# First block of a mixture layer with whole float32 products in place of split halves, on one Trainium2 core

## The chip, the cores and the metric

The kernel runs on one core of a Trainium2 chip. The metric is the device time of one execution in microseconds. Three runs of the kernel before gave 1545.82, 1546.03 and 1547.47 us, so its median is 1546.03 us.

## What is computed

Everything is float32. Attention comes first: keys and values are averaged over groups of 8 positions, so each of the 8 x 8 heads (576 queries, 64 wide) sees 72 keys. Its output is x, 4608 tokens by 512. Two feed-forward layers follow; the second takes the output of the first:

```python
h = np.maximum(np.maximum(x @ w1, x @ w2), x @ w3)   # 512 -> 768, three experts
y = h @ w_out                                        # 768 -> 512
h = np.maximum(y @ w_in, 0.0)                        # 512 -> 2048
return h * h @ w_out2                                # 2048 -> 512
```

The weights come from the host as 64-bit floats, read as pairs of 32-bit words.

## The kernel before, in words

**Split products.** A float32 operand is kept as two halves of the type float32r: hi is the operand rounded by a ScalarE (ACT) copy, lo the difference between the operand and hi. A product is then three float32r matmuls that add up in one PSUM bank, hi x hi, hi x lo and lo x hi (`PARTS`). The function `split` (L124, through `split_to`, L120) does it with one ACT copy (L121) and one subtraction (L122), on VectorE (DVE) or, where it is told so, on GpSimd (POOL).

**Weights of the first layer.** There are 24 weight tiles of 128 x 512: 18 for the three experts (`w1_t[f, e]`, 6 values of f, 3 experts) and 6 for the second product (`wo1_t[kk]`). The function `weights` (L161) makes each: `load_raw` (L128) loads 512 KB of 64-bit floats through SyncE's DMA queue into one of four buffers that turn in a ring (`place`, L113), `convert` (L136) makes float32 of it in a tile of three (tag "row") by two ACT operations (L148, L149) and two DVE operations (L150, L153), and `split` makes the halves, the subtraction on POOL. The raw buffers are shared with loads of keys (`load_k`) and values (`load_v`).

**The first layer by blocks.** The tokens go in 12 blocks of 384. `moe1(j)` (L453) makes one block in 22 steps: 18 steps (f, e) of 4 x 3 matmuls of 384 columns each (L465), with a running maximum over the experts (L471 on ACT, L473 on DVE) and a split of h after the third (L475); then 4 steps of 6 x 3 matmuls (L484), whose result goes out to DRAM (L490, L491). Three PSUM banks (`mm_ps`) serve these steps. The input of a block is four tiles x[kk], kk = 0 to 3, one for each pair of heads.

**Attention by pieces.** `attend` (L307) makes x for one pair and one run of tokens: load, `prepare` (q split, L330, on POOL for the first two blocks), `softmax` (L332: scores L344, maximum L346, exponentials L349, reciprocal L354, and a scaling on POOL, L355), `transpose` (L362: L370, and the halves of the transposed tile, L372 and L373), `values` (L375: L385 for the first batch, L395 to L399 for the others, ending with the split of x, L389 or L400).

**Order.** Each piece of work has a due time in steps in the list `todo`; `run` (L494) emits it in that order. A scheduler with a model of the chip then orders each engine's own instructions, so an engine takes them in an order fixed beforehand and waits at the head of its queue. Attention of block j is due before `moe1(j)` and beside `moe1(j-1)`. Weight loads of the first layer are due from step -12 on, 0.9 of a step apart:

```python
todo.append((0.9 * (NE * f + e) - 12, functools.partial(load_w1, f, e)))
todo.append((0.9 * (NE * KF1 + kk) - 12, functools.partial(load_wo1, kk)))
```

**The second layer.** Its weights are prepared during blocks 2 to 10 and stored in DRAM. From about 785 us on, the second layer runs alone (L600, L645).

Of the kernel before, what the change touches and what calls it, by code (L numbers as in the profile page):

```python
# [14 lines left out]
AF = mybir.ActivationFunctionType  # L15
ALU = mybir.AluOpType
# [4 lines left out]
P = 128  # L21
# [6 lines left out]
KD = DM // P  # L28
FF1 = 768
KF1 = FF1 // P  # L30
FF2 = 2048
KF2 = FF2 // P
NE = 3
# [7 lines left out]
PARTS = ((0, 0), (0, 1), (1, 0))  # L41
# [3 lines left out]
STEPS = NE * KF1 + KD  # L45
# [20 lines left out]
NATURAL = 1  # L66

LIGHT = 2

# [8 lines left out]
def as_f32(ap):  # L80
    return ap.bitcast(F32)
# [3 lines left out]
def attention_moe_kernel(ctx: ExitStack, tc: tile.TileContext, q, k, v, vn, w1, w2, w3, wo1, wi2, wo2, out):  # L85
    nc = tc.nc
# [11 lines left out]
    for sign, base in ((1, POOL * MID), (-1, POOL - 1 - POOL * MID)):  # L98
        nc.gpsimd.affine_select(
            out=sums, in_=sums, compare_op=ALU.is_ge, fill=0.0, base=base,  # L100
# [12 lines left out]
    def place(kind):  # L113
        if shared[0]:
            turns["both"] += 1
            return f"raw{turns['both'] % 4}"
        turns[kind] += 1
        return f"raw{2 * kind + turns[kind] % 2}"

    def split_to(hi, lo, src, engine):  # L120
        nc.scalar.activation(hi, src, AF.Copy)  # L121
        engine.tensor_tensor(out=lo, in0=src, in1=as_f32(hi), op=ALU.subtract)  # L122

    def split(hl, src, engine=nc.vector):  # L124

        split_to(hl[:, 0], hl[:, 1], src, engine)

    def load_raw(raw_pool, src, after=None):  # L128

        raw = raw_pool.tile([P, 512, 2], I32, tag=place(0), name="wraw", bufs=1)  # L130
        if after is not None:
            nc.gpsimd.tensor_copy(as_f32(raw[:1, 0, :1]), after[:1, :1])
        nc.sync.dma_start(out=raw.rearrange("p a b -> p (a b)"), in_=src.bitcast(I32))
        return raw

    def convert(raw_pool, raw, after=None):  # L136

        low, high = raw[:, :, 0], raw[:, :, 1]
        a = raw_pool.tile([P, 512], I32, tag="row", name="wbits", bufs=3)
        if after is not None:
            nc.gpsimd.tensor_copy(as_f32(a[:1, :1]), after[:1, :1])
        nc.scalar.activation(as_f32(a), as_f32(high), AF.Abs, scale=REBIAS)  # L148
        nc.scalar.activation(low, low.bitcast(U32), AF.Copy, scale=LOW_SCALE, bias=LOW_BIAS)  # L149
        nc.vector.scalar_tensor_tensor(  # L150
            out=a, in0=a, scalar=3, in1=low, op0=ALU.logical_shift_left, op1=ALU.bitwise_or
        )
        nc.vector.scalar_tensor_tensor(  # L153
            out=a, in0=high, scalar=-0x80000000, in1=a, op0=ALU.bitwise_and, op1=ALU.bitwise_or
        )
        return as_f32(a)
# [2 lines left out]
        return raw.rearrange("p a b -> p (a b)").rearrange("p (c a) -> p c a", c=2).bitcast(F32R)  # L159

    def weights(pool, raw_pool, src, name, tag=None):  # L161
        w = pool.tile([P, 2, 512], F32R, name=name, tag=tag or name)
        split(w, convert(raw_pool, load_raw(raw_pool, src)), nc.gpsimd)
        return w


    s1 = ctx.enter_context(ExitStack())
# [89 lines left out]
    x_t = {}  # L257
# [10 lines left out]
    def score_tiles(n):  # L268
        m = P if n % P == 0 else n // 2
        return [(c, m) for c in range(0, n, m)]  # L270

    def attention(j):

        x_t[j] = [None] * NPAIR
        n_tiles = sum(NPAIR * len(score_tiles(n)) for _, _, n, _ in pieces(j))
        pace = (STEPS - 1) / n_tiles
        at = (j - 1) * STEPS + pace / 2 - (LAG_T + LAG_V + LEAD_X)
        for b, s0, n, t in pieces(j):
            if s0 == 0 and b < NATURAL:
                tiles = []  # L280
                when = at - pace / 2 + LAG_T + LAG_V if t else at + pace / 2
                todo.append((when - LEAD_LOAD, lambda b=b, tiles=tiles: tiles.extend(load_natural(b))))
                todo.append((when, lambda tiles=tiles: pool_v(tiles)))
            for p in range(NPAIR):
                load, prepare, softmax, transpose, values = attend(j, b, s0, n, p, t)
                todo.append((at - LEAD_LOAD, load))
                todo.append((at - LEAD_PREP, prepare))
                tiles = score_tiles(n)
                if j < LIGHT:
                    todo.append((at, functools.partial(softmax, tiles)))  # L290
                for c, m in tiles:
                    if j >= LIGHT:
                        todo.append((at, functools.partial(softmax, [(c, m)])))
                    todo.append((at + LAG_T, functools.partial(transpose, c, m)))
                    at += pace
                todo.append((at - pace + LAG_T + LAG_V, values))
# [10 lines left out]
    def attend(j, b, s0, n, p, t):  # L307

        kr, vr, qr, qs, pt, sms = [], [], [], [], [], {}
        first, light = s0 == 0, j < LIGHT  # L310

# [63 lines left out]
        def values():  # L375
            if t == 0:
                x_t[j][p] = x_p.tile([P, 2, T1], F32R, tag="x", name="x")
            x = x_t[j][p][:, :, t : t + n]
            hi, lo = pt[0][:, 0, :, :n], pt[0][:, 1, :, :n]
            if b < NATURAL:  # L380
                av = av_ps.tile([P, T1], F32, tag="av0", name="av0")[:, :n]
                for i, (h, z, rhs) in enumerate(
                    (h, z, rhs) for h in range(2) for z, rhs in ((h, hi), (h, lo), (3 + h, hi))
                ):
                    nc.tensor.matmul(  # L385
                        av, lhsT=vst[:, p, z : z + 2].rearrange("p a d -> p (a d)"), rhs=rhs[:, h],
                        start=(i == 0), stop=(i == 5),
                    )
                split(x, av)  # L389
                return  # L390
            xf = xf_p.tile([P, T1], F32, tag="xf", name="xf")[:, :n]
            for h in range(2):
                av = av_ps.tile([P, T1], F32, tag=f"av{h}", name=f"av{h}")[:, :n]
                lhsT = vst[:, p, 2 * h : 2 * h + 2].rearrange("p a d -> p (a d)")
                nc.tensor.matmul(av, lhsT=lhsT, rhs=hi[:, h], start=True, stop=False)  # L395
                nc.tensor.matmul(av, lhsT=lhsT, rhs=lo[:, h], start=False, stop=True)  # L396
                r, o = slice(h * D, (h + 1) * D), slice((1 - h) * D, (2 - h) * D)
                nc.scalar.activation(xf[r], av[o], AF.Copy)
                nc.vector.tensor_tensor(out=xf[r], in0=av[r], in1=xf[r], op=ALU.add)  # L399
            split(x, xf)  # L400
# [3 lines left out]
    w1_t, wo1_t = {}, {}  # L404
# [47 lines left out]

    def moe1(j):  # L453

        x = x_t.pop(j)
        hs = []
        for f in range(KF1):
            hm = t_p.tile([P, T1], F32, tag="hm", name="hm")
            h = h_p.tile([P, 2, T1], F32R, tag="h", name="h")
            for e in range(NE):  # L460
                ps = mm_ps.tile([P, T1], F32, tag="ps", name="ps")
                n = 0
                for kk in range(KD):
                    for a, c in PARTS:
                        nc.tensor.matmul(  # L465
                            ps, lhsT=w1_t[f, e][:, a, kk * P : (kk + 1) * P], rhs=x[kk][:, c],
                            start=(n == 0), stop=(n == 3 * KD - 1),
                        )
                        n += 1
                if e == 0:  # L470
                    nc.scalar.activation(hm, ps, AF.Copy)  # L471
                else:
                    nc.vector.tensor_tensor(out=hm, in0=ps, in1=hm, op=ALU.max)  # L473
                if e == NE - 1:
                    split(h, hm)  # L475
                yield
            hs.append(h)
            now[0] = hm
        for d in range(KD):
            ps = mm_ps.tile([P, T1], F32, tag="ps", name="ps")  # L480
            n = 0
            for kk in range(KF1):
                for a, c in PARTS:
                    nc.tensor.matmul(  # L484
                        ps, lhsT=wo1_t[kk][:, a, d * P : (d + 1) * P], rhs=hs[kk][:, c],
                        start=(n == 0), stop=(n == 3 * KF1 - 1),
                    )
                    n += 1
            ys = t_p.tile([P, T1], F32, tag="ys", name="ys")
            nc.scalar.activation(ys, ps, AF.Copy)  # L490
            nc.scalar.dma_start(out=y_dram[j][d], in_=ys)  # L491
            yield
# [6 lines left out]
    def add_moe1(j):  # L499
        steps = moe1(j)  # L500
        todo.extend((j * STEPS + i, functools.partial(next, steps, None)) for i in range(STEPS))

    todo = []
# [3 lines left out]
            todo.append((0.9 * (NE * f + e) - 12, functools.partial(load_w1, f, e)))  # L507
    for kk in range(KF1):
        todo.append((0.9 * (NE * KF1 + kk) - 12, functools.partial(load_wo1, kk)))
    for j in range(NB1 - 1):  # L510
        add_moe1(j)
        attention(j + 1)
# [216 lines left out]
```

## Time and profile before

| | |
|---|---|
| median of three runs | 1546.03 us |
| the profiled execution, its own time | 1546.39 us |
| its span, first to last instruction | 1544.7 us |
| PE (TensorE matmul) busy | 1509.4 us, 98% |
| DVE busy | 948.2 us, 61% |
| ACT busy | 623.5 us, 40% |
| POOL busy | 199.4 us, 13% |
| DMA | 200.87 MB, mean 130 GB/s |

PE is the matmuls and PEld the weight loads into the array, which run beside them. A matmul's busy time contains the tail in which its results drain, so matmuls that follow each other closely overlap in the table of means, and a rate is better read from start to start or from a long unbroken run. PEclk is the granted clock of TensorE as a share of 2.4 GHz; 0.50 is 1.2 GHz. SPq is SyncE's queue of DMA issues. An arrow in the idle column names what ended the idle time. A wait for several things is put down to the one that came last.

### The profile page before, as it was taken

Reading aid. Unit: us, or ns where it says so; the run is one execution under the profiler, and the core shown is the slowest. Engines: PE = TensorE matmul, PEld = TensorE weight load, DVE = VectorE, ACT = ScalarE, POOL = GpSimd, SP = SyncE. Lnnn points to the kernel's source line nnn. Section 1 sums busy time; section 2 is a strip of 40 time slices with the busy share of each in tenths; the row PEclk is TensorE's granted clock in tenths of the full one; section 3 lists DMA queues with packets and bytes.
Section 4 is the critical chain, followed back from the end, with each engine's and each line's share of the span. In section 5 each row is a group of like instructions: output and inputs, shape, how many; then the busy total and the mean of one; then the engine's idle time right before and its main releaser. Section 6 shows DMA issues by size and latency. Waiting matters only on the chain.

```text
span 1544.7 us, 25098 instructions
## 1 busy us (share of the span) xinstructions
PE 1509.4 (98%) x9290; PEld 1413.8 (92%) x9290; DVE 948.2 (61%) x1991; ACT 623.5 (40%) x1772; POOL 199.4 (13%) x303
## 2 busy tenths in 40 slices
PE   6899999999999999999999999999999999999998
PEld 4789999999999999999999898988989888999987
DVE  6895678776776767755427555455655546464544
ACT  7875566656666556654212212121212112121211
POOL 5541122222222121322000000000000000000000
PEclk7799999999999999999999999999999999999999
DMA  7552234434334332323475424333333433343331
GB/s 226 159 172 68 76 105 149 145 95 143 122 119 143 97 132 99 102 77 123 135 289 208 150 109 164 110 121 123 112 137 124 150 123 108 111 150 109 137 109 69
DMA packets 80858, 200.87 MB, mean 130 GB/s; under 512 B 9024, under 2 KB 32576, under 8 KB 80736
## 3 DMA queue, kind: packets, MB, share of 16 engines
q1 hardware_dynamic: 73824, 189.83, 36.1%
q10 hardware_dynamic: 6912, 9.44, 1.7%
q8 instruction: 74, 1.21, 0.3%
q14 instruction: 48, 0.39, 0.1%
HBM read 157.29 MB, written 41.94 MB: 129 GB/s over the span
## 4 chain that ended last, share of the span: by engine, by line
PE 85%; DVE 5%; DMA 5%; ACT 2%; issue 2%; SPq 0%; POOL 0%; DVEq 0%; ACTq 0%; POOLq 0%
PE ps L465 25%; PE acc L645 25%; PE ps L600 21%; PE ps L484 9%; PE sc L344 2%; DMA out_dram<-o 2%; PE tr L370 2%; DMA wraw<-in_w_dram 1%; PE av L396 1%; PE av L395 1%; DVE wbits L153 1%; DMA vr<-in_v_dram 1%; DMA wraw<-in_wo_dram 1%; DMA kq<-in_k_dram 1%; DVE wbits L150 0%
## 5 line engine op out<-in xcount | busy, mean ns | idle before, releaser
L465 PE MATMUL ps<-x,w 128*128 128x384 f32 x2592 | 507.6, 343 | 1.8 <-DVE x L122 1.0
L465 PEld LDWEIGHTS ps<-x,w 128*128 128x128 f32 x2592 | 451.1, 191 | 3.9 <-DVE x L122 2.0
L645 PE MATMUL acc<-wo2s,g 128*128 128x512 f32 x1728 | 412.5, 391 | 0.0
L600 PEld LDWEIGHTS ps<-y,wi2s 128*128 128x128 f32 x3024 | 370.4, 188 | 12.5 <-PE ps L600 3.4
L600 PE MATMUL ps<-y,wi2s 128*128 128x256 f32 x3024 | 376.8, 280 | 2.8 <-DVE s L629 2.2
L645 PEld LDWEIGHTS acc<-wo2s,g 128*128 128x128 f32 x1728 | 316.2, 188 | 62.6
L121 ACT ACTIVATE g<-c 128x512 fp32r<-128x512 f32 x144 | 90.8, 630 | 410.4 <-DVE c L611 403.6
L617 DVE TENSOR_TENSOR s<-ps,s 128x512 f32<-128x512 f32 x72 | 49.8, 692 | 262.2 <-PE ps L600 261.6
L484 PE MATMUL ps<-h,wo 128*128 128x384 f32 x864 | 165.2, 339 | 0.5 <-DVE hm L473 0.4
L484 PEld LDWEIGHTS ps<-h,wo 128*128 128x128 f32 x864 | 148.9, 188 | 1.3 <-DVE hm L473 0.7
L617 DVE TENSOR_TENSOR c<-ps,s 128x512 f32<-128x512 f32 x144 | 99.0, 688 | 24.9 <-PE ps L600 21.7
L355 POOL TENSOR_TENSOR ss<-ss,st 128x144 f32<-128x144 f32 (+3 forms) x144 | 74.2, 517 | 308.7 <-DVE st L354 238.6
L473 DVE TENSOR_TENSOR hm<-ps,hm 128x384 f32<-128x384 f32 x144 | 79.5, 552 | 54.2 <-PE ps L465 50.3
L349 ACT ACTIVATE ss<-sc,st 128x72 f32<-128x72 f32 (+1 forms) x320 | 98.3, 314 | 33.3 <-DVE st L346 30.8
L122 DVE TENSOR_TENSOR g<-c,g 128x512 fp32r<-128x512 f32 x144 | 98.8, 686 | 17.3 <-ACT g L121 16.4
L611 DVE SCALAR_TENSOR_TENSOR c<-c 128x512 f32<-128x512 f32 x144 | 99.0, 688 | 2.2
L373 DVE TENSOR_TENSOR pt<-tr,pt 72x256 fp32r<-72x256 f32 (+1 forms) x160 | 61.5, 387 | 52.6 <-ACT pt L372 51.2
L344 PEld LDWEIGHTS sc<-kbd,qs 128*128 128x128 f32 (+1 forms) x480 | 73.3, 191 | 12.3 <-issue 5.3
L344 PE MATMUL sc<-kbd,qs 128*128 128x144 f32 (+1 forms) x480 | 73.9, 269 | 9.2 <-ACT kbd L195 5.3
L372 ACT ACTIVATE pt<-tr 72x256 fp32r<-72x256 f32 (+1 forms) x160 | 56.4, 355 | 58.9 <-PE tr L370 57.4
L370 PE MATMUL tr<-ident,ss 128*72 128x128 f32 (+1 forms) x320 | 59.2, 271 | 13.9 <-DVE pt L373 8.8
L349 ACT ACTIVATION_READ_ACCUMULATOR ss<-sc,st 128x1 f32 (+1 forms) x320 | 63.4, 198 | 0.0
(78 smaller groups left out, 1247.0 us busy)
## 6 DMA issues: line engine op xcount, KB each, us to landing
wo2s<-wo_dram SPq DMA_DIRECT2D x144, 512.0 KB
wi2s<-wi_dram SPq DMA_DIRECT2D x24, 512.0 KB
wraw<-in_wo_dram SPq DMA_DIRECT2D x22, 512.0 KB
wraw<-in_w_dram SPq DMA_DIRECT2D x18, 512.0 KB
y_dram<-ys ACTq DMA_DIRECT2D x48, 192.0 KB
out_dram<-o SPq DMA_DIRECT2D x36, 256.0 KB
wraw<-in_wi_dram SPq DMA_DIRECT2D x16, 512.0 KB
wi_dram<-wraw SPq DMA_DIRECT2D x16, 512.0 KB
```

The source lines that it names most:

```text
L121: nc.scalar.activation(hi, src, AF.Copy)
L122: engine.tensor_tensor(out=lo, in0=src, in1=as_f32(hi), op=ALU.subtract)
L344: nc.tensor.matmul(src[:, i], lhsT=lhsT, rhs=kbd[:, p, l], start=(n == 0), stop=(n == 2))
L349: nc.scalar.activation(ss[:, i, h], src[:, i, h], AF.Exp, bias=st[:, 0, i, h : h + 1], accum_out=st[:, 1, i, h : h + 1],)
L370: nc.tensor.transpose(tr[:, h, :m], sms[c][:, h], ident[:m, :m])
L465: nc.tensor.matmul(ps, lhsT=w1_t[f, e][:, a, kk * P : (kk + 1) * P], rhs=x[kk][:, c], start=(n == 0), stop=(n == 3 * KD - 1),)
L473: nc.vector.tensor_tensor(out=hm, in0=ps, in1=hm, op=ALU.max)
L484: nc.tensor.matmul(ps, lhsT=wo1_t[kk][:, a, d * P : (d + 1) * P], rhs=hs[kk][:, c], start=(n == 0), stop=(n == 3 * KF1 - 1),)
L600: nc.tensor.matmul(bank[:, u * HT : (u + 1) * HT], lhsT=wi2_t[2 * gr + u][i][:, a, o + kk * P : o + (kk + 1) * P], rhs=y_t[j][m][:, c, kk] ...
L611: nc.vector.scalar_tensor_tensor(out=c, in0=c, scalar=0.0, in1=c, op0=ALU.max, op1=ALU.mult)
L617: nc.vector.tensor_tensor(out=c, in0=bank, in1=other, op=ALU.add)
L645: nc.tensor.matmul(acc_t[j][2 * half + i], lhsT=g[:, a, u * HT + i * P : u * HT + (i + 1) * P], rhs=wo2_t[j, 4 * gr + 2 * u + h][:, c], st ...
```

## The change

For block 0 alone (`WHOLE = 1`), both products of the first layer take the unsplit float32 operands, so a product is one float32 matmul in place of three float32r matmuls. x and h of block 0 are no longer split: the ACT copy of x stays (as a plain float32 copy), and the maximum of the third expert writes h. A weight's float32 tile is copied by a DMA from the "row" tile into the lo half of its place, and used from there. `split_weights` makes the halves later and in place: due half a step behind the step of block 0 that uses the weight for the experts' tiles, and from step 21.5 on, one a step, for the six others.

```diff
     def weights(pool, raw_pool, src, name, tag=None):
         w = pool.tile([P, 2, 512], F32R, name=name, tag=tag or name)
-        split(w, convert(raw_pool, load_raw(raw_pool, src)), nc.gpsimd)
+        nc.sync.dma_start(out=as_f32(w[:, 1]), in_=convert(raw_pool, load_raw(raw_pool, src)))
         return w
+    def split_weights(w):
+        split(w, as_f32(w[:, 1]), nc.gpsimd)
+    def sum_products(out, pairs, whole):
+        if whole:
+            parts = [(as_f32(l[:, 1]), as_f32(r[:, 0])) for l, r in pairs]
+        else:
+            parts = [(l[:, a], r[:, c]) for l, r in pairs for a, c in PARTS]
+        for n, (l, r) in enumerate(parts):
+            nc.tensor.matmul(out, lhsT=l, rhs=r, start=(n == 0), stop=(n == len(parts) - 1))
...
-                split(x, av)
+                if j < WHOLE:
+                    nc.scalar.activation(as_f32(x[:, 0]), av, AF.Copy)
+                else:
+                    split(x, av)
...
-        x = x_t.pop(j)
+        x, whole = x_t.pop(j), j < WHOLE
...
+                sum_products(ps, [(w1_t[f, e][:, :, kk * P : (kk + 1) * P], x[kk]) for kk in range(KD)], whole)
+                last = e == NE - 1
                 if e == 0:
                     nc.scalar.activation(hm, ps, AF.Copy)
                 else:
-                    nc.vector.tensor_tensor(out=hm, in0=ps, in1=hm, op=ALU.max)
-                if e == NE - 1:
+                    to = as_f32(h[:, 0]) if whole and last else hm
+                    nc.vector.tensor_tensor(out=to, in0=ps, in1=hm, op=ALU.max)
+                if last and not whole:
                     split(h, hm)
...
+            sum_products(ps, [(wo1_t[kk][:, :, d * P : (d + 1) * P], hs[kk]) for kk in range(KF1)], whole)
...
+    for n in range(NE * KF1):
+        todo.append((n + 0.5, lambda n=n: split_weights(w1_t[divmod(n, NE)])))
+    for kk in range(KF1):
+        todo.append((STEPS - 0.5 + kk, lambda kk=kk: split_weights(wo1_t[kk])))
```

## Rows read from the trace of the kernel before

**Rows 1.** The page, busy tenths in 40 slices of 38.6 us.

```profile
PE   6899999999999999999999999999999999999998
```

**Rows 2.** Busy time by stretch: us, PE, PEld, DVE, ACT, POOL, clock, DMA share, GB/s.

```profile
13.00:61.20 48.20, 33.13 (x152) 26.21 (x151) 39.20 (x82) 40.53 (x142) 29.42 (x27) 0.70 0.59 190
61.20:126.70 65.50, 61.90 (x358) 58.36 (x358) 60.04 (x129) 49.66 (x156) 28.94 (x27) 0.94 0.48 154
126.70:734.80 608.10, 604.35 (x3729) 595.49 (x3729) 415.67 (x1101) 361.49 (x1178) 135.64 (x239) 1.00 0.34 112
```

**Rows 3.** Timeline of PE, and of DVE at the last piece of x.

```profile
34.38 1.31 PE L465 MATMUL ps<-x,w 128*128 128x384 f32 x3
36.01 2.29 PE L465 MATMUL ps<-x,w 128*128 128x384 f32 x6 [0.32 <-DVE x L122]
...
61.20 0.52 DVE L122 TENSOR_TENSOR x<-av,x 128x384 fp32r<-128x384 f32 x1
...
126.69 1.21 PE L465 MATMUL ps<-x,w 128*128 128x384 f32 x6
```

**Rows 4.** Matmuls by line, window 61.2 to 126.7 us.

```profile
L465 PE MATMUL ps<-x,w 128*128 128x384 f32 x189 | 38.8, 357 | 0.2
L484 PE MATMUL ps<-h,wo 128*128 128x384 f32 x72 | 13.6, 339 | 0.4 <-DVE hm L473 0.4
```

**Rows 5.** The chain that ended last, in the last block of the first layer.

```profile
734.80 37.44 PE ps L465 x216
772.24 12.48 PE ps L484 x72
```

**Rows 6.** The float32 matmuls of L250: single records, then the line's group.

```profile
9.25 1.06 PE L250 MATMUL vp<-natural,sums 128*72 128x512 f32 x1
...
10.10 1.06 PE L250 MATMUL vp<-natural,sums 128*72 128x512 f32 x1
...
12.17 0.59 PE L250 MATMUL vp<-natural,sums 128*72 128x512 f32 x1
...
12.60 0.59 PE L250 MATMUL vp<-natural,sums 128*72 128x512 f32 x1
...
L250 PE MATMUL vp<-natural,sums x10: 589/620/1100, 8.4 to 14.0; 128*72 128x512 f32 x8, 64*72 64x512 f32 x2
```

**Rows 7.** Groups by line in the window 13 to 61.2 us.

```profile
L122 POOL TENSOR_TENSOR w<-wbits,w 128x512 fp32r<-128x512 f32 x10 | 14.5, 1456 | 7.4 <-ACT w L121 7.4
L121 ACT ACTIVATE w<-wbits 128x512 fp32r<-128x512 f32 x10 | 6.2, 634 | 2.2 <-DVE wbits L153 2.2
```

**Rows 8.** The chain before 61.2 us: start, us, what.

```profile
22.18 5.00 DMA vr<-in_v_dram
...
29.09 4.62 DMA wraw<-in_w_dram
...
35.05 0.51 ACT w L121
...
38.55 3.60 DMA vr<-in_v_dram
...
45.91 0.47 DVE x L122
...
47.34 5.00 DMA wraw<-in_w_dram
...
54.79 0.52 ACT w L121
...
56.76 1.04 ACT w L121 x2
```

**Rows 9.** A small DVE operation beside POOL's subtractions of weights, and its like.

```profile
58.52 2.52 POOL L122 TENSOR_TENSOR w<-wbits,w 128x512 fp32r<-128x512 f32 x2
...
59.49 1.58 DVE L353 TENSOR_SCALAR st<-st 96x4 f32<-96x4 f32 x1 [0.84 <-ACT ss L349]
63.74 0.16 DVE L353 TENSOR_SCALAR st<-st 96x4 f32<-96x4 f32 x1
```

More of the change, by code (lines that the diff above doesn't have):

```diff
@@ L68 @@
 LIGHT = 2
+WHOLE = 1
 REBIAS = 2.0**-112
@@ L461, in moe1 @@
                 ps = mm_ps.tile([P, T1], F32, tag="ps", name="ps")
[L462 to L469, printed above, removed]
+                sum_products(ps, [(w1_t[f, e][:, :, kk * P : (kk + 1) * P], x[kk]) for kk in range(KD)], whole)
+                last = e == NE - 1
                 if e == 0:
@@ L480, in moe1 @@
             ps = mm_ps.tile([P, T1], F32, tag="ps", name="ps")
[L481 to L488, printed above, removed]
+            sum_products(ps, [(wo1_t[kk][:, :, d * P : (d + 1) * P], hs[kk]) for kk in range(KF1)], whole)
             ys = t_p.tile([P, T1], F32, tag="ys", name="ys")
```

## The prediction

> **What bounds the kernel now.** Start with the strip of busy tenths [rows 1]: PE is full in every slice but the first two and the last. The table by stretch says the same in numbers [rows 2]: from 126.7 us on, PE is busy 604.35 of 608.10 us and later more than 99%, at a granted clock of 1.00. So the run behind 126.7 us is a sum of PE work, and what the change can win or lose lies before it. The timeline gives that point its meaning [rows 3]: at 126.69 us the first matmuls of block 1 start, so block 0 ends there.
>
> The start-up has two parts, divided by one event: at 61.20 us DVE makes the last piece of block 0's x [rows 3]. Before it a step can do only the part of its sum whose x is there, and three PSUM banks hold three steps. In the 48.2 us before it PE is busy 33.1 us at a mean clock of 0.70, while ACT, DVE and POOL are busy 40.5, 39.2 and 29.4 us [rows 2]: a chain through several engines, none of them full. In the 65.5 us behind it PE is busy 61.9 and DVE 60.0 us [rows 2]: both nearly full. The end is thus the time of the last x plus the work of block 0 behind it.
>
> **PE's part behind the last x.** Of block 0's 216 + 72 float32r matmuls 189 + 72 = 261 lie here, busy 38.8 + 13.6 = 52.4 us [rows 4]. Run without a break they take 37.44/216 = 12.48/72 = 0.1733 us each [rows 5], so 261 x 0.1733 = 45.2 us; 7 us are surplus (cold clock, tails, waits). PE is idle for 65.5 - 61.9 = 3.6 us, and 61.9 - 52.4 = 9.5 us go to attention.
>
> The price of a whole float32 product has one witness, the pooling matmul of L250: five instructions in the code, ten records in the trace [rows 6]. Each of 512 columns takes two records, 0.43 us from start to start (12.17 to 12.60) once the engine has run for some us, and 0.85 us (9.25 to 10.10) before. The two are one to two, as 1.2 and 2.4 GHz are. For 384 columns I scale by columns: 2 x 0.43 x 384/512 = 0.645 us at the faster rate, against 3 x 0.1733 = 0.52 us for the three it replaces: 0.125 us more for each of 96 products, 12 us over block 0. Bounds: 0.52 us (no dearer than what it replaces) and 1.29 us (the slower rate); the L250 rows are the same operation, so I take 0.645.
>
> Behind the last x lie 261/3 = 87 products: 87 x 0.645 = 56.1 us. With attention 9.5 us that is 65.6 us without any loss: as long as the whole 65.5 us now. Today's loss is 7 + 3.6 = 10.6 us. Weights and DVE press less after the change, so I keep 6 to 7 of it: the clock still starts cold after a sparse stretch, and PE still waits a little for attention of block 1. Part two: 72 us, **+6.5 us** (bounds +2 for nearly no loss, +10.5 for all of it).
>
> **What comes off the way to the last x.** In the 48.2 us before 61.2 us ten weights are split: ten ACT copies, 6.2 us, for one of which ACT waits 2.2 us, and ten POOL subtractions, 14.5 us [rows 7]. They are not saved but put behind the step that uses each weight. The chain holds 0.51 + 0.52 + 1.04 = 2.1 us of those copies and 0.47 us of a DVE half of x [rows 8], which goes too. DVE also works faster beside an idle POOL: an operation of 0.16 us took 1.58 us while POOL subtracted weights from 58.52 to 61.04 us [rows 9]. I give that 1.4 us, one such delay on the path: together 4 us earlier. The upper bound is all of it, 6.2 + 2.2 + 3 x 0.47 + 1.4 = 11 us.
>
> The page "SBUF — State Buffer" of the Trainium skill (section "SBUF: two separate sides") says that a GpSimd operation and a VectorE operation with two SBUF inputs exclude each other for a whole instruction. By that, every subtraction that leaves could free DVE for up to 1.46 us, 14.6 us for the ten in place of my 1.4, which is what the faster rival below would need; the row of 1.58 us agrees in one place.
>
> **What is added on that way.** Each weight gets a DMA of 256 KB in place of the split. The trace has no such copy; the nearest rows are loads of 288 KB (3.60 and 5.00 us) and 512 KB (4.62 and 5.00 us) [rows 8]. I take 4.3 us, between the two of nearest size; it replaces about 0.63 + 1.46 us of split, so a weight comes 2.2 us later. The cover is the lead of weights: ten are done at 61.2 us, where three are in use, and behind it a step takes 4 x 0.645 us and its share of attention, 9.5/22 = 0.4 us, so 3.0 us. Without that lead it would cost 2.2 us per weight.
>
> All DMAs of this stage but the small y stores stand in SP's queue. A copy waits there for its L153, with loads of raw weights, keys, values and q behind it. Those weight, key and value loads already wait for a raw buffer that an earlier L153 frees, so the new wait costs them mostly the issue. But traffic rises: 24 copies are 6 MB, and the four DMA waits on the chain (5.00 + 4.62 + 3.60 + 5.00 = 18.2 us [rows 8]) may grow. Bounds 0 and 5 us, a quarter longer each; I take 1 us. The three early groups of products cost 3 x 1.29 = 3.9 us at the slow rate where nine float32r took 1.31 + 2.29 = 3.6 us [rows 3]; PE is idle 15 us there, which covers it. So the last x comes at about **58 us, 3 us earlier**.
>
> **Edits that I cost at nothing.** The later ACT copies and subtractions of w1 fall into block 0 behind their step. POOL then waits for PE's step n with the scaling of later softmax pieces behind it; their transposes are due three steps, some 9 us, later. The six of wo1 fall into block 1, whose second layer needs them 18 steps later, and POOL is busy 135.64 of 608.10 us [rows 2]. The six missing splits of h free DVE of some 4 us; since PE binds, that gives nothing. If DVE were still late, its saving would count and PE's loss would shrink by as much.
>
> **The sum.** +6.5 - 3 = +3.5 us on the profiled execution of 1546.39 us, 0.36 us above the median. From the median, 1546.03 + 3.5 = 1549.5 us.
>
> **The rivals.** *Faster: the last x comes early.* The place is the chain to 61.2 us. If nearly all of the 11 us leaves it, and the loss behind it is small (+3 us), the end is 8 us earlier: 1538 us, and with 9 us of relief 1540. It decides from 6.5 us of relief on. For it: ACT and POOL lose 6.2 of 40.5 and 14.5 of 29.4 us, and the long DVE operation [rows 9]. Against it: the chain itself shows only 2.6 us of this work, and its DMA waits stay.
>
> *No change: the two parts cancel.* Relief of 5 to 8 us and a loss of 5 to 7: within 3 us of 1546.
>
> *Much slower: the copies hold up the loads.* If each of the four DMA waits grows by a quarter, the last x comes at 61.2 - 4 + 5 = 62 us, and with today's full loss behind it the sum is +1 + 10.5 = +11.5 us: 1557.5 us. The page "DMA: Bandwidth & Descriptors" of the Trainium skill (section "Queues, rings and completion order") has descriptors of one queue consumed in ring order on each DMA engine, so that a copy issued behind loads waits for them. For this rival: a 288 KB load took 3.60 us once and 5.00 us another time [rows 8]. Against it: the DMA share is only 0.59 and 0.48 in the two stretches [rows 2].
>
> *It does not do what it says.* If the products ran as one record each, PE would have 87 x 0.32 = 28 us less to do behind the last x, and DVE, 60 of 65.5 us full, would bind: 4 us less DVE work and the relief before it, some -6 us, 1540. Against it: L250 has plain float32 operands and two records each [rows 6].
>
> **How the numbers follow.** Chances: forecast (+1 to +8 us) 0.42, faster rival 0.22, cancelling 0.18, much slower 0.15, not as said 0.03. A measurement of this kernel can tell about 0.2%, 3.1 us, from no change. Slower by more: 0.27 of the forecast and the slow rival, 0.42. Within: 0.15 of the forecast, 0.16 of the cancelling case, 0.03 of the others, 0.34. Faster: 0.24. The forecast's own range is 1547 to 1554; with the other cases up to 2 in 10 left out it is 1539 to 1559.
>
> **What would show it.** Right: L465 and L484 in block 0 as two records for each product, 0.32 us from start to start, without a break behind the last x; that x at about 58 us; PE busy over 95% between it and block 1; DVE with idle time there; block 1 starting near 130 us, and everything behind it as before. Wrong: PE idle for several us behind the last x (DVE, DMA or POOL binds on), the last x before 54 or behind 62 us, or a stretch behind block 1's start that differs by more than a us or two.

## The result, and the profile after

The changed kernel takes 1554.05 us, the median of four runs (1553.84 to 1555.23), against 1545.92 us before (1542.72 to 1547.47): a ratio of 1.0056 [1.0041, 1.0071]. The change makes it slower by about 8 us. The forecast had the side and the main mechanism; its size, +3.5 us, was less than half. The profiled execution took 1554.13 us, its span 1552.4 us, 7.7 us more than before.

Page of the changed kernel: PE's line, then its strip of busy tenths.

```profile
PE 1518.1 (98%) x9194; PEld 1396.4 (90%) x9194; DVE 944.2 (61%) x1981; ACT 620.6 (40%) x1766; POOL 194.9 (13%) x303
...
PE   6899999999999999999999999999999999999998
```

The picture is that of [rows 1]: the shares of PE and DVE are the same, and but for the longer span nothing on the page tells that the kernel lost time. It has to be read from the stages, as in [rows 2]. Busy time by stretch after the change (us, PE, PEld, DVE, ACT, POOL, clock, DMA share, GB/s):

```profile
13.00:57.25 44.25, 31.09 (x136) 21.30 (x136) 32.87 (x75) 37.17 (x135) 13.53 (x16) 0.75 0.74 242
57.25:130.94 73.69, 70.92 (x274) 44.27 (x274) 57.67 (x115) 47.88 (x147) 35.94 (x32) 0.96 0.59 200
130.94:741.21 610.27, 605.65 (x3733) 596.70 (x3733) 419.76 (x1107) 363.11 (x1188) 139.64 (x243) 0.99 0.34 112
```

Timeline of the changed kernel: the last piece of block 0's x (an ACT copy now), unbroken runs of its products, and the start of block 1. They answer to [rows 3].

```profile
56.77 0.48 ACT L407 ACTIVATE x<-av 128x384 f32<-128x384 f32 x1
...
59.28 3.87 PE L181 MATMUL ps<-x,w 128*128 128x384 f32 x6
...
69.86 5.35 PE L181 MATMUL ps<-x,w 128*128 128x384 f32 x16
75.05 0.33 PE L387 MATMUL tr<-ident,ss 96*72 96x96 f32 x2
...
130.94 0.91 PE L181 MATMUL ps<-x,w 128*128 128x384 f32 x4
```

The last x is complete at 56.77 + 0.48 = 57.25 us, where it was 61.20 + 0.52 = 61.72 us before: 4.5 us earlier. Block 1 starts at 130.94 instead of 126.69 us: 4.25 us later. What lies between has grown from 64.97 to 73.69 us, by 8.7 us. Sixteen records fill 69.86 to 75.05 us, 0.324 us each, so a product of two records takes 0.65 us.

Groups of the changed kernel from 57.25 to 130.94 us (busy, mean ns of one | idle just before, and what ended it):

```profile
L181 PE MATMUL ps<-x,w 128*128 128x384 f32 x126 | 46.1, 508 | 1.1 <-DVE hm L488 1.1
L126 POOL TENSOR_TENSOR w<-w 128x512 fp32r<-128x512 f32 x18 | 26.0, 1453 | 8.3 <-PE ps L181 8.3
L181 PE MATMUL ps<-h,wo 128*128 128x384 f32 x48 | 16.5, 491 | 0.0
```

The 126 + 48 = 174 records are 87 products of two, where [rows 4] had 189 + 72 = 261. All 18 subtractions of the experts' weights lie here now, and none before the last x, where [rows 7] had ten. Groups of the changed kernel from 13 to 57.25 us:

```profile
L154 DVE SCALAR_TENSOR_TENSOR wbits<-wbits,wraw 128x512 int32<-128x512 int32 x10 | 7.0, 718 | 1.0 <-ACT wraw L153 1.0
L157 DVE SCALAR_TENSOR_TENSOR wbits<-wraw,wbits 128x512 int32<-128x512 int32 x10 | 6.6, 679 | 0.0
...
L125 ACT ACTIVATE w<-w 128x512 fp32r<-128x512 f32 x8 | 4.9, 630 | 1.2 <-DMA w<-wbits 1.2
```

Eight of the ten ACT copies still run before the last x: the scheduler puts them in as soon as the DMA copy has landed. What left this stretch is POOL's work (29.42 us in [rows 2], 13.53 now) and some of DVE's (39.20, now 32.87). What PE waits for between 57.25 and 130.94 us, in the changed kernel (us in all, times, longest):

```profile
PE ps L181 <- DVE hm L488: 1.1, 1, 1.1
PE tr L387 <- DVE pt L390: 1.0, 1, 1.0
PE av L415 <- DVE xf L419: 0.4, 1, 0.4
PE sc L361 <- ACT ss L366: 0.3, 1, 0.3
```

That is 2.8 us in all: no DMA and no POOL stands in the list, and in this execution PE binds behind the last x, as forecast. The second execution of the same kernel, in the table below, is less clear: there PE is busy for 72.06 of 78.22 us, and its longest wait is for DVE's transposed halves:

```profile
PE tr L387 <- DVE pt L390: 4.2, 2, 3.2
```

Each of the two kernels was profiled once more, and the two executions of one kernel tell how finely these numbers can be read:

| us | before | before again | change | change again |
|---|---|---|---|---|
| last x complete | 61.7 | 60.9 | 57.3 | 55.2 |
| block 1 starts | 126.7 | 126.4 | 130.9 | 133.4 |
| between them | 65.0 | 65.5 | 73.7 | 78.2 |
| block 1 | 59.5 | 59.5 | 61.0 | 61.0 |
| block 7 | 65.0 | 63.8 | 66.9 | 65.6 |
| blocks 1 to 10 | 607.9 | 606.1 | 610.3 | 609.0 |
| block 11, second layer and the end | 810.1 | 811.7 | 811.2 | 811.8 |
| span | 1544.7 | 1544.2 | 1552.4 | 1554.2 |

By the means of the two, block 0 ends 5.7 us later, blocks 1 to 10 take 2.6 us longer, and the rest, whose code is the same, 0.6 us: 8.9 us of span. One execution of the change starts block 1 2.5 us later than the other, so a difference of that size between two single executions says nothing about the start-up. Three of the kernels below turn out to run the same start-up again (one that of the kernel before, two that of the change); with them the spread of the change's start of block 1 is 4.4 us.

### The profile page after: what moved, and what is told of

The parts are those of the page before. It is cut to its first block, busy times and chain, and to the rows that moved or that the text cites. A ratio compares the mean times of both kernels' runs of the same rounds, so it can differ in the third digit from the quotient of the medians.

```text
span 1552.4 us, 24960 instructions
## 1 busy us (share of the span) xinstructions
PE 1518.1 (98%) x9194; PEld 1396.4 (90%) x9194; DVE 944.2 (61%) x1981; ACT 620.6 (40%) x1766; POOL 194.9 (13%) x303
## 4 chain that ended last, share of the span: by engine, by line
PE 54%; DMA 3%; DVE 1%; issue 0%; ACT 0%; SPq 0%; DVEq 0%; ACTq 0%
PE acc L657 24%; PE ps L612 21%; PE ps L181 8%; DMA out_dram<-o 2%; DVE c L629 0%; DVE s L641 0%; DMA wraw<-in_wo_dram 0%; PE tr L387 0%; ACT o L669 0%; PE sc L361 0%; PE av L416 0%; SPq L670 0%; PE av L415 0%; DVE s L629 0%; DVE c L623 0%
## 5 line engine op out<-in xcount | busy, mean ns | idle before, releaser
L181 PE MATMUL ps<-x,w 128*128 128x384 f32 x2520 | 514.2, 352 | 5.5 <-ACT x L407 4.4
L181 PEld LDWEIGHTS ps<-x,w 128*128 128x128 f32 x2520 | 437.1, 190 | 21.8 <-ACT x L407 4.7
L181 PEld LDWEIGHTS ps<-h,wo 128*128 128x128 f32 x840 | 145.4, 188 | 5.6 <-DVE h L488 0.2
L488 DVE TENSOR_TENSOR hm<-ps,hm 128x384 f32<-128x384 f32 x138 | 76.2, 552 | 48.9 <-PE ps L181 46.0
L361 PE MATMUL sc<-kbd,qs 128*128 128x144 f32 (+1 forms) x480 | 79.1, 276 | 8.9 <-ACT kbd L212 5.2
L361 PEld LDWEIGHTS sc<-kbd,qs 128*128 128x128 f32 (+1 forms) x480 | 73.7, 191 | 14.8 <-issue 6.3
L387 PE MATMUL tr<-ident,ss 128*72 128x128 f32 (+1 forms) x320 | 59.3, 270 | 10.8 <-DVE pt L390 10.3
L363 DVE TENSOR_REDUCE st<-sc 128x2 f32<-128x144 f32 (+3 forms) x144 | 45.5, 316 | 30.3 <-PE sc L361 26.6
```

What stands on the lines that cost most here:

```text
L181: nc.tensor.matmul(out, lhsT=l, rhs=r, start=(n == 0), stop=(n == len(parts) - 1))
L361: nc.tensor.matmul(src[:, i], lhsT=lhsT, rhs=kbd[:, p, l], start=(n == 0), stop=(n == 2))
L488: nc.vector.tensor_tensor(out=to, in0=ps, in1=hm, op=ALU.max)
```

## The experiments

The theory after this profile: PE's dearer products behind the last x cost more than the earlier x brings, and some of the rest comes from the late splits, which crowd DVE and POOL in block 0. Rivals: the DMA copies hold the weights back; the start-up costs nothing and the loss lies elsewhere.

**PE's price taken away.** Three float32r matmuls per product in block 0, as before, but all three of the unsplit operands; the rest is the change.

```diff
-            parts = [(as_f32(l[:, 1]), as_f32(r[:, 0])) for l, r in pairs]
+            parts = [(l[:, 1], r[:, 0]) for l, r in pairs for _ in PARTS]
...
-                    nc.scalar.activation(as_f32(x[:, 0]), av, AF.Copy)
+                    nc.scalar.activation(x[:, 0], av, AF.Copy)
...
-                    to = as_f32(h[:, 0]) if whole and last else hm
+                    to = h[:, 0] if whole and last else hm
```

> The changed kernel, but block 0 does each product as three float32r matmuls of the unsplit operands in place of one float32 matmul (so block 0's products come out three times too large and rounded: it leaves the exact product out). Weight copies and late splits stay as in the change. Theory (the price of the float32 product on PE, 0.125 us for each of the 87 products behind the last x, is what the change lost): the last x stays at 56 to 59 us, the stretch from it to block 1 falls by 9 to 12 us, block 1 starts at 119 to 123 us and the whole takes 1542 to 1546 us. Rival (copies and late loads hold block 0, PE only fills the time): block 1 still starts at 128 us or later and the whole stays above 1550 us.

Measured: 1542.21 us, ratio 0.9959 [0.9944, 0.9973]. The total is where the theory had it, but not by its way. Two windows of this kernel, the stretch behind the last x and ten of its us:

```profile
59.32:128.19 68.87, 61.71 (x366) 57.74 (x365) 60.42 (x115) 47.84 (x146) 40.02 (x32) 0.96 0.63 209
...
70.00:80.00 10.00, 9.93 (x63) 9.79 (x64) 9.97 (x22) 6.10 (x21) 6.70 (x5) 1.00 0.88 287
```

The stretch falls only from 73.69 to 68.87 us, by 4.8 us (by 9.35 us against the 78.22 us of the second execution), where PE's work falls by 70.92 - 61.71 = 9.2 us: PE is idle 7.2 us now, against 2.8 in the change, and DVE is full in places (9.97 of 10 us). PE's longest waits in this stretch are for DVE:

```profile
PE tr L387 <- DVE xf L419: 2.2, 1, 2.2
PE tr L387 <- DVE pt L390: 1.5, 2, 1.2
```

Of the total's gain 7.3 us come from block 7, 59.6 us here and 66.9 us in the change; of that below. So without the price of the float32 products block 1 still starts at 128.2 us, just on the rival's side (128 us or later) and behind the 126.7 us of before. That is too close to decide by one execution: with the same products a later kernel starts block 1 at 124.4 us.

**The copies doubled.**

```diff
-        nc.sync.dma_start(out=as_f32(w[:, 1]), in_=convert(raw_pool, load_raw(raw_pool, src)))
+        row = convert(raw_pool, load_raw(raw_pool, src))
+        nc.sync.dma_start(out=as_f32(w[:, 0]), in_=row)
+        nc.sync.dma_start(out=as_f32(w[:, 1]), in_=row)
```

> The changed kernel with every weight copied twice, into both halves of its place (24 more DMAs of 256 KB on SP's queue; the first copy is overwritten later). Theory (the copies are hidden by the lead of the weights): 1552 to 1557 us, the last x at 56 to 59 us. Rival (copies delay the loads behind them and so the last x or the weights): at least 4 us more than the change, 1558 us or above, the last x at 60 us or later, and then the first copies cost about as much.

Measured: ratio 1.0055 [1.0038, 1.0072], that of the change. The last x comes at 57.9 us, the stretch takes 75.3 us, between the change's 73.7 and 78.2. To within the interval, some 2 us, the copies are hidden.

**More PE work in the kernel before.** A fourth matmul, lo x lo, in every product of block 0.

```diff
+        parts = PARTS + ((1, 1),) * (j == 0)
...
-                    for a, c in PARTS:
+                    for a, c in parts:
```

> The kernel before, with a fourth float32r matmul, lo x lo, in every product of block 0: 96 more matmuls, 87 of them behind the last x, 87 x 0.173 = 15 us of PE work, and nothing else changed. Theory (PE binds behind the last x, with up to some 7 us of slack in waits): 8 to 15 us more than before, 1554 to 1561 us. Rival (DVE's conversions of weights bind block 0 of the kernel before, PE has room): at most 4 us more, up to 1550 us.

Measured: ratio 1.0057 [1.0042, 1.0072]. Behind the last x, in this kernel:

```profile
62.01:140.45 78.44, 75.11 (x447) 72.95 (x448) 58.91 (x122) 48.98 (x144) 30.38 (x25) 0.96 0.41 128
```

87 more matmuls of 0.1733 us are 15.1 us; the stretch grows from 65.0 to 78.4 us, by 13.4 us. In the kernel before, PE work behind the last x counts nearly in full. The total rises by less, 9.3 us, mostly because block 7 takes 59.6 us in this kernel and 65.0 in the one before.

**The weight path alone.** The change with `WHOLE = 0`: all blocks use split halves, the weights come by copy and are split in place, four steps ahead of their use.

```diff
-WHOLE = 1
+WHOLE = 0
...
-        todo.append((n + 0.5, lambda n=n: split_weights(w1_t[divmod(n, NE)])))
+        todo.append((n - 4, lambda n=n: split_weights(w1_t[divmod(n, NE)])))
...
-        todo.append((STEPS - 0.5 + kk, lambda kk=kk: split_weights(wo1_t[kk])))
+        todo.append((NE * KF1 - 4 + 0.5 * kk, lambda kk=kk: split_weights(wo1_t[kk])))
```

> The products of the kernel before in all blocks (three float32r matmuls of split halves, x and h split), with the weight path of the change: copy by DMA, split in place, but due four steps ahead of the weight's use in place of half a step behind it. Theory (the way to the last x gains from fewer subtractions on POOL, and the loss of the change is PE's price alone): the last x at 57 to 60 us, the stretch behind it 64 to 67 us as before, the whole 1541 to 1545 us. Rival (what the change gains before the last x needs the splits to go behind the use, not just behind the conversion): within 2 us of before, 1544 to 1548 us.

Measured: 1550.86 us, ratio 1.0023 [1.0013, 1.0033]. Both expectations were too low. The windows before and behind the last x, then the longest wait of PE before it:

```profile
13.00:68.91 55.91, 36.89 (x155) 29.58 (x154) 44.40 (x87) 43.60 (x154) 28.73 (x28) 0.63 0.68 226
68.91:134.51 65.60, 60.10 (x355) 56.81 (x354) 57.25 (x117) 45.77 (x137) 29.22 (x24) 0.95 0.60 198
```

```profile
PE tr L387 <- DVE pt L390: 14.2, 5, 4.0
```

and what ACT's copies of the weights wait for before the last x:

```profile
L125 ACT ACTIVATE w<-w 128x512 fp32r<-128x512 f32 x11 | 7.0, 633 | 6.1 <-DMA w<-wbits 6.1
```

The stretch is that of before, 65.6 us, but the last x comes 7 us later than before: POOL has its subtractions back (28.73 us busy), PE waits for DVE's transposed halves, and ACT waits 6.1 us for the DMA copies. So the DMA path by itself brings no relief. That the relief needs splits behind the first use fits this, but it isn't shown alone: this kernel also splits x and h again.

**The same two kernels again.** Both unchanged.

> The kernel before, unchanged, for a second trace. If the stall of block 7 (PE waits 1.9 us for an exponential, and the clock falls behind it) belongs to the order of the instructions, block 7 again takes 64 to 66 us where blocks 2 to 6 take about 60.5; if it is chance, it takes about 60. If the second layer's time differs between executions for its own reasons, its span differs by more than 1 us from 810.1 us (784.56 us less the 734.64 us of block 11 counted in).

> The changed kernel, unchanged, beside the others of this call, for a second trace and more times. Last x at 57 to 58 us, block 1 at 130 to 132 us, block 7 again 66 to 68 us, 1.004 to 1.007 of before.

Measured: 1545.95 us (one run) and 1555.01 us, ratio 1.0052 [1.0037, 1.0067]. The table above has them beside the first pair. Block 7's long time is there in both repeats; the start of block 1 at 133.4 us was expected at 130 to 132.

**The late splits due in block 1.** With the change's products, and once more with the three unsplit ones (the edits of the first experiment with this one).

```diff
-        todo.append((n + 0.5, lambda n=n: split_weights(w1_t[divmod(n, NE)])))
+        todo.append((STEPS + n - 4, lambda n=n: split_weights(w1_t[divmod(n, NE)])))
...
-        todo.append((STEPS - 0.5 + kk, lambda kk=kk: split_weights(wo1_t[kk])))
+        todo.append((STEPS + 10 + kk, lambda kk=kk: split_weights(wo1_t[kk])))
```

> The changed kernel with the late splits put off into block 1: each weight of the experts split four steps ahead of its use there, those of w_out from step 10 of block 1 on. Theory (PE's price binds block 0, what POOL and DVE do beside it costs at most PE's waits of 2.8 us): the last x as in the change, the stretch from it to block 1 shorter by 1 to 4 us, 70 to 73 us; the whole 1550 to 1555 us. Rival (DVE and POOL, not PE, bind block 0 in the change too): the stretch falls below 69 us.

> The same late splits, with three float32r matmuls of the unsplit operands in block 0 in place of one float32 matmul (block 0's products come out three times too large and rounded: the exact product is left out). Theory (in the run with three unsplit products DVE was the bound behind the last x, full from 70 to 120 us beside 40 us of POOL work, and the subtractions on POOL were what slowed it): the stretch from the last x to block 1, 68.9 us there, falls by 4 to 8 us, and PE's share in it rises. Rival (conversions alone fill DVE): it falls by less than 2 us.

Measured: 1555.80 us, ratio 1.0057 [1.0042, 1.0072], and 1545.07 us, ratio 0.9993 [0.9983, 1.0002]. The stretch behind the last x, first with float32 products:

```profile
56.12:132.92 76.80, 70.29 (x275) 44.18 (x274) 60.00 (x115) 47.74 (x146) 33.02 (x32) 0.97 0.57 192
```

and with the three unsplit ones:

```profile
56.12:124.43 68.31, 62.23 (x365) 59.32 (x365) 60.36 (x115) 48.40 (x146) 36.82 (x31) 0.94 0.64 211
```

Neither stretch falls against its own twin (73.7 to 78.2, and 68.9 us). But this isn't a test of the theory. POOL's subtractions of the experts' weights in the two stretches, again with float32 products first:

```profile
L126 POOL TENSOR_TENSOR w<-w 128x512 fp32r<-128x512 f32 x18 | 23.7, 1324 | 11.0 <-PE ps L181 11.0
L126 POOL TENSOR_TENSOR w<-w 128x512 fp32r<-128x512 f32 x18 | 27.0, 1510 | 12.6 <-PE ps L181 8.7 <-ACT wbits L152 1.9 <-PE sc L361 1.9
```

All 18 still run before block 1, as in the change: the edit moved the due times, but not the splits. The first kernel's trace has the instructions of every engine in the very order of the change, from start to end, so it is a third execution of the change; in the second the order differs somewhat from that of its twin, but the splits are not moved out of block 0 either. Whether late splits crowd block 0 stays untested. What the pair does give is the price of the float32 products, since both kernels reach the last x at 56.12 us: 76.80 - 68.31 = 8.5 us.

**Float32 in the experts' products alone.** The last experiment's first kernel, with the six weights of the second product and h split as before and those 24 products back at three matmuls.

```diff
-        wo1_t[kk] = weights(w_p, raw_p, wo1[kk], f"wo1_{kk}", spare[kk])
+        wo1_t[kk] = halves(w_p, raw_p, wo1[kk], f"wo1_{kk}", spare[kk])
...
-                if last and not whole:
+                if last:
                     split(h, hm)
...
-            sum_products(ps, [(wo1_t[kk][:, :, d * P : (d + 1) * P], hs[kk]) for kk in range(KF1)], whole)
+            sum_products(ps, [(wo1_t[kk][:, :, d * P : (d + 1) * P], hs[kk]) for kk in range(KF1)], False)
```

> The changed kernel with the late splits in block 1, and float32 products only in the first 18 steps of block 0: w_out and h are split as in the kernel before, so 24 of the 96 products go back to three float32r matmuls. Theory (each float32 product costs PE 0.125 us, and PE binds): the stretch from the last x to block 1, 76.8 us with the same late splits, falls by 2 to 4 us, to 72.8 to 74.8 us; the whole 1551 to 1554 us. Rival (the splits of h and w_out that come back cost as much on DVE): it falls by less than 1 us or rises.

Measured: 1559.91 us, ratio 1.0089 [1.0075, 1.0103], slower than the change. Less PE work, by 24 x 0.125 = 3 us, and yet a stretch of 78.0 us, within the spread of the change's own, and a total some 4 us above the experiment before. The theory's fall of 2 to 4 us is not there, so the rival held. That DVE is the reason is argued from PE's largest wait, for which the kernel with all products in float32 has 3.6 us:

```profile
PE tr L392 <- DVE pt L395: 5.7, 2, 4.4
```

**One unsplit matmul per product.** As the first experiment, with a single float32r matmul for each product of block 0.

```diff
-            parts = [(as_f32(l[:, 1]), as_f32(r[:, 0])) for l, r in pairs]
+            parts = [(l[:, 1], r[:, 0]) for l, r in pairs]
```

> The changed kernel with one float32r matmul of the unsplit operands for each product of block 0 (its products are rounded: the exact product is left out), a quarter of the float32 product's PE time, 87 x 0.47 = 41 us less PE work behind the last x. It shows what else holds block 0. Theory (behind PE comes DVE, full with conversions of weights and with attention of block 1, as in the run with three unsplit products, which took 68.9 us from the last x to block 1): the stretch falls only to 60 to 67 us. Rival (PE is the only bound): it falls below 50 us.

Measured, one run: 1541.90 us beside 1546.93 before; block 7 takes 59.6 us here. The stretch, and what PE waits for in it:

```profile
57.34:127.95 70.61, 52.27 (x207) 45.15 (x206) 66.58 (x141) 53.46 (x175) 43.92 (x36) 0.57 0.62 205
```

```profile
PE ps L181 <- DMA wo<-wbits: 5.9, 4, 3.1
PE av L415 <- DVE x L126: 5.2, 1, 5.2
PE av L402 <- DVE x L126: 3.1, 1, 3.1
```

One short matmul stands here for each pair of long records, and the stretch is 70.6 us all the same, above the 60 to 67 us of the theory. DVE is busy 66.58 us, partly with work drawn forward (141 operations here, 115 in the change), PE waits for it and for copies, and the granted clock is 0.57, so a slow PE may have a part in the length too. What is shown is that below three float32r matmuls the stretch no longer follows PE's price: in none of the three kernels with products cheaper than float32 does block 0 end before 124 us, and in two it ends at 128; the kernel before ended it at 126.7. Of the kernels that keep block 0's full product, none is faster than the one before.

**Block 7.** Both kernels take about 64 to 67 us for a block that takes 60 elsewhere. Here attention of block 8 was moved by a step in the kernel before, and by a step the other way in the change.

```diff
+        at += 1 * (j == 8)
```

> The kernel before, with the attention of block 8 due one step later. In the order of PE's instructions that breaks a clump of 22 attention matmuls in a row in block 7 (none of the first layer's between them) into at most 12. Theory (the slow block 7 of the kernel before, 65.0 and 63.8 us in its two traces, is that clump, and the clock that falls behind PE's wait): block 7 takes 60 to 61.5 us, blocks 0 to 6 as before, the whole 0.9965 to 0.9985 of before, 3 to 5 us less. Rival (block 7 is long for another reason, its weights for the second layer): 63 us or more, the whole within 0.999 to 1.001.

```diff
+        at += -1 * (j == 8)
```

> The changed kernel with the attention of block 8 due one step earlier, which breaks the same clump in its order (20 matmuls) into at most 12. Theory: block 7 takes 60 to 61.5 us in place of 66.9 and 65.6, blocks 0 to 6 as in the change, the whole 1.0005 to 1.0025 of before; against the kernel before without its clump it is then 5 to 8 us slower, which is what block 0 and block 1 alone cost. Rival: block 7 still takes over 64 us.

Measured: 1547.54 us, ratio 1.000 [0.999, 1.001], block 7 at 66.0 us; and 1552.90 us, ratio 1.0039 [1.0026, 1.0053], block 7 at 63.6 us, where 60 to 61.5 were expected of both. The rival held in the first; the second lies between. A clump broken into 12 is thus not enough. In the first the wait only changed its name, from ACT's exponentials to DVE's transposed half:

```profile
PE tr L371 <- DVE pt L374: 2.4, 1, 2.4
```

The wait is there in six of the variants and the two kernels, and absent (59.6 us) with three unsplit matmuls, with one, with the fourth matmul, and with the weight path alone. These four have no edit in common that touches block 7. They do share one thing in the order of PE's instructions: their longest run of attention matmuls in block 7 is 8, where the slow ones have 20 to 22, or 12 in the two kernels here. So the length of the clump goes with the wait; as no run shortened it to 8 and left the rest alone, whether it is the cause isn't shown.

Up to 460 us these two kernels run the instructions in the order of the kernel before and of the change, so each is one more execution of its start-up: last x at 62.3 and 58.0 us, block 1 at 128.9 and 135.3 us.

## Why the prediction was right, and where its size was off

**PE's price: right.** 174 records of 0.324 us, 0.65 us per product where 0.645 was forecast from [rows 6]. 87 x 0.645 = 56.1 us, and the groups show that number of products behind the last x.

**The last x: right to 2 us, partly by luck.** 4.5 us earlier in the first pair, 5.0 by the means of the three executions of the start-up before and the four of the change, where 3 were forecast. The forecast read 2.1 us of ACT copies off the chain [rows 8]; eight of these copies still run there. What left the way is POOL's subtractions, and the weight path alone, which has them back, makes the last x 11.7 us later than in the change; with its other differences that is a sign, not a proof, of where the relief came from. The rule of "SBUF — State Buffer" in the Trainium skill (section "SBUF: two separate sides") is borne out in kind, not in size. DVE's two conversions went from 773 and 755 ns (ten each before the last x, in the groups of before) to 718 and 679 ns, which is 1.3 us over ten weights. That this is close to the 1.4 us taken from [rows 9] is chance: the forecast meant one delay of another operation, and that one has a single tensor input, so its row is no witness for a rule of two. The single conversions are better witnesses. From 13 us to the start of block 1, in both kernels, none without a POOL operation beside it took over 0.70 us; most of those beside one took no longer either, but some did, up to 2.96 us before and 2.68 us after. The last x came 4.5 us earlier, not 14.6.

**What the copies cost: 1 us was charged, none is seen.** Doubling them changed nothing beyond the spread, and the rival of held-up loads is out: the last x came at 57.25 us, not 62. They are also shorter than the 4.3 us of the estimate. The chain of waits of the kernel with one matmul per product, where PE did wait for some of them, has four, of 2.3 to 3.8 us; the shortest and the longest are

```profile
109.14 2.30 DMA wo<-wbits
...
120.66 3.77 DMA wo<-wbits
```

By the ring order of "DMA: Bandwidth & Descriptors" in the Trainium skill (section "Queues, rings and completion order") loads behind a copy would have waited for it; no run here shows a cost of that. ACT does wait for the copies themselves ahead of the last x: 1.2 us in the change, and 6.1 us in the weight path alone, whose splits come sooner.

**The loss behind the last x: the step that was mis-sized.** "I keep 6 to 7 of it" was to be the rest of today's 10.6 us, since "weights and DVE press less after the change". The profile after has 73.69 us = 56.1 of products + 8.3 of attention (70.92 - 46.1 - 16.5) + 9.3 of loss, and this is the shortest of four executions: the others take 76.8, 77.3 and 78.2 us. By the means of the three executions before and the four of the change, PE is idle for 4.9 and 5.2 us, and its records of these products are busy for 6.7 and 7.2 us longer than at their unbroken rate (0.1733 us, and 0.645 us for two): 11.6 us of loss before, 12.4 us after. Nothing of it went, though DVE does press less (57.67 of 73.69 us in the first profile, 59.51 of 64.97 before). The sign of PE busy for over 95% held in the first profile (96%) and in none of the other three (92 to 93%). A part of the loss is seen in the windows right behind the last x of the first profile:

```profile
57.00:60.00 3.00, 3.00 (x14) 2.70 (x15) 1.48 (x7) 3.00 (x14) 0.66 (x1) 0.50 1.01 375
60.00:62.00 2.00, 2.00 (x5) 1.09 (x4) 1.60 (x3) 1.73 (x6) 1.10 (x1) 0.50 0.21 78
64.00:66.00 2.00, 2.00 (x7) 1.20 (x7) 1.91 (x4) 2.00 (x8) 2.00 (x3) 1.00 0.14 55
```

The clock is at 1.2 GHz there until 62 us at least, and at full rate from 64 us on. Six records fill 3.87 us in the timeline, twice their 1.94 us: some 2 us. The rest I read as the tails at each change between products and attention; no run took them apart. Term by term in the first pair: stretch +8.7 where +6.5 was forecast, last x -4.5 where -3 was, together +4.25 for +3.5. By the means of all executions: stretch +10.8, just beyond the bound of +10.5 for all of today's loss, last x -5.0, together +5.8. The sum for the start-up is within 2.3 us only because a stretch forecast 4.3 us too short stands against a relief forecast 2.0 us too small; that is luck. The kernels with three unsplit products, 68.9 and 68.3 us behind the last x, divide the +10.8: 7.9 us are the price of the float32 products, and 2.9 us come with the rest of the change, which no run takes apart.

**"Everything behind it as before": wrong by about 2.6 us, over blocks 1 to 10.** Block 1 takes 61.0 for 59.5 us in both pairs, of which 0.5 us are a wait for DVE's transposed half and most of the rest attention drawn into it (38 score matmuls for 33, 26 transposes for 24). Blocks 2 to 6 together give back about 1 us. Block 7 takes 1.9 us more. Windows of the changed kernel there:

```profile
500.00:502.00 2.00, 0.86 (x6) 0.48 (x6) 1.50 (x6) 1.90 (x8) 0.00 (x0) 1.00 0.00 0
502.00:504.00 2.00, 0.57 (x4) 0.42 (x4) 1.86 (x8) 1.93 (x10) 0.74 (x1) 0.78 0.19 23
504.00:506.00 2.00, 2.00 (x9) 1.83 (x10) 1.46 (x7) 1.24 (x8) 0.85 (x2) 0.50 0.45 121
506.00:508.00 2.00, 2.00 (x9) 2.00 (x9) 1.60 (x7) 1.62 (x5) 0.43 (x1) 0.50 0.27 101
508.00:510.00 2.00, 2.00 (x11) 1.83 (x9) 1.97 (x5) 0.18 (x1) 0.00 (x0) 0.51 0.36 98
```

and of the kernel before:

```profile
496.00:498.00 2.00, 0.39 (x2) 0.13 (x2) 1.88 (x8) 1.90 (x8) 0.00 (x0) 1.00 0.00 0
498.00:500.00 2.00, 1.66 (x11) 1.51 (x12) 2.00 (x9) 1.60 (x9) 0.36 (x1) 0.94 0.37 98
500.00:502.00 2.00, 2.00 (x8) 2.00 (x7) 1.70 (x6) 1.91 (x9) 0.80 (x2) 0.50 0.75 171
502.00:504.00 2.00, 2.00 (x12) 2.00 (x11) 1.86 (x5) 0.30 (x1) 0.43 (x1) 0.70 0.33 107
504.00:506.00 2.00, 2.00 (x14) 2.00 (x13) 1.96 (x5) 1.95 (x5) 0.29 (x2) 1.00 0.69 164
```

Both have a stretch in which PE is mostly idle, then one at half the clock; the change has 4 us of the first and some 6 of the second, the kernel before about 2 and 3. The table by stretch [rows 2] gave a clock of 1.00 and PE over 99% busy for 608 us, and means over a stretch that long hide it: a mean says what a stretch costs, not that each of its blocks costs the same or that a new instruction order will leave them alone.

**The rivals.** The faster one asked for 6.5 us of relief and a small loss; relief was 4.5 to 5.7 and the whole loss stayed. "As if one record each" was priced at -6 us on the ground that DVE binds; the kernel with one matmul per product, which does just that to PE, ends block 0 at 127.95 us, no earlier than before (126.4 to 128.9 us in three executions). That price was wrong, and that this kernel's total is 5 us below the one before comes mostly from block 7.

**What stays open.** What makes the wait in block 7; whether late splits crowd block 0; why the start-up of one kernel differs by up to 4.4 us between executions; how much of block 1's 1.5 us is order and how much is work.

## What to carry to other kernels

Price an instruction that gets dearer at the place where its engine binds, and price what it relieves on the chain that it leaves; here some 8 us of PE stood against some 5 us of an earlier start. Work moved out of a crowded stage comes back in the next, so find what sets the floor there before counting the gain: kernels with cheap products still ended block 0 at 124 to 128 us. A small edit in a kernel with a fixed instruction order can shift a wait hundreds of us later, so compare the stages, not the totals, before giving a few us to the edit. An edit can also leave that order as it was, so compare the order of the two traces before taking a run for a test.

## What was not expected of the hardware

A pause of PE costs more than itself. In block 7 of the kernel before one wait of 1.89 us (to 498.29 us) is followed, some 2 us later, by a window at 0.50 and one at 0.70 of full clock, though PE is busy throughout; in the change two thin windows (0.86 and 0.57 of 2 us busy) are followed by 6 us at 0.50. PE is idle for 2.1 to 2.6 us in the slow blocks, and they take 64 to 67 us, where kernels whose PE is never idle there take 59.6. And where PE has little to do in block 0 (one matmul per product: 52.27 of 70.61 us busy) its mean clock is 0.57, and its matmuls with x average 483 ns, against 357 ns in the kernel before [rows 4]: part of the time taken from it came back as slower work.
